# A two-level Strassen product: another order of the outer products, and the last two outputs stored in quarters

## The chip, the cores and the metric

The kernel runs on one core of a Trainium2 chip. The metric is the device time of one execution in microseconds (us), the median of several. The engines named here are TensorE (PE, matrix products, with its weight loads shown as PEld), VectorE (DVE, element-wise work), ScalarE (ACT), GpSimd (POOL) and SyncE (SP, which here only issues DMA transfers). A run before the change took 942.15 us (median of 3, from 942.0 to 943.19).

## The reference

A retention layer without softmax, then a feed-forward block with a squared ReLU. Everything is float32.

```python
# q, k, v: (8, 8, 576, 64)
scores = scale * np.matmul(q, k.transpose(0, 1, 3, 2))
ret = scores * Dmat[None, :, :, :]          # decay by position, zero above the diagonal
attn = np.matmul(ret, v)
x = attn.transpose(0, 2, 1, 3).reshape(4608, 512)
h = np.maximum(x @ w_in, 0.0)               # w_in: (512, 2048)
out = h * h @ w_out                         # w_out: (2048, 512)
```

The case is about the last line, called the second product here: g = h*h, 4608 tokens by 2048, times w_out, 2048 by 512.

## The kernel before, in words

Retention and the first product (x @ w_in) take the first 547 us, and the second product the rest. Tokens stand along the free dimension throughout, so outputs are computed transposed.

**The second product is Strassen's scheme in Winograd's form, twice, one inside the other.** One level replaces the eight products of a 2 x 2 block product by seven, listed in `PRODUCTS` (L27): A11·B11, S2·T2, S1·T1, A12·B21, S3·T3, S4·B22, A22·T4. S1 to S4 are sums of quarters of the left side: S1 = A21 + A22, S2 = S1 - A11, S3 = A11 - A21, S4 = A12 - S2. T1 to T4 are sums of quarters of the right side (the weights), made in earlier stages.

**Outer level.** The tokens are worked in six groups. A group has seven *steps*, one for each outer product, in the order of `OUTER` (L38), so there are N_K = 42 steps, k = 0 to 41, and j = k % 7 is the place in the group. Before, the order was S1, A11, S2, A12, S4, S3, A22. The left operand of a step is a buffer A(k) of 128 x 3072 elements, and there are four such buffers, used in turn (k % 4). A11, S1, A12, S3 and A22 were computed with the first product, are kept in DRAM (`g_dram`) and fetched by `fetch_g` in two halves, LOW and HIGH, one over the rows 0 to 3, the other over 4 to 7 of the buffer's eight. S2 and S4 are not kept: `made` (L969 to L976) subtracts two buffers that are there, in four quarters, each one DVE instruction of 768 elements per partition (L975). In the order of its list, quarter 0 is (LOW, RIGHT), 1 is (HIGH, RIGHT), 2 is (LOW, LEFT) and 3 is (HIGH, LEFT). For the inner level these are A21, A22, A11 and A12 of that operand.

**Inner level.** `inner(k, i)` is inner product i of step k: eight matmul passes of 128 x 192 in the trace (L1053), 1.30 us. The inner sums S1 to S4 are made by `inner_sum` (L992), each one DVE instruction of 768 elements. The products' results are combined from PSUM by DVE and ACT: p1 (ACT, L1060), u2 (DVE, L1062), p15 (L1064), then the four quarters of the step's result r (ACT L1066, DVE L1068, L1070, L1072).

**The order in the loop** (L1117 to L1149) is written by hand; each engine works its own list in that order. A step of the loop interleaves the first four inner products of step k with the last three of step k - 1. On PE it reads: inner(k,0), inner(k-1,4), inner(k,1), inner(k-1,5), inner(k,2), inner(k-1,6), inner(k,3), 9.1 us in all. The three passes of the inner loop (e = 0, 1, 2) are called thirds of a step below. DVE's list in a step is, third by third:

- e = 0: the quarter of r from inner(k-1,4); u2; what `extra(0)` holds; S1 of step k+1; the transposes of an output that leaves.
- e = 1: the quarter of r from inner(k-1,5); p15; S3 and S4 of step k; what `extra(1)` holds.
- e = 2: the quarter of r from inner(k-1,6); S2 of step k+1; the outer additions of step k-1; what `extra(2)` holds.

`extra` takes the quarters of `made` (the table `extras`, L1121) and, until they are used up, steps of `sums_0` (L1001), which loads, adds (L1016) and stores sums for one block of tokens that the first product left undone. At the end of a step SP gets the fetches of half a buffer for step k+3 and half for step k+4 (L1148, L1149).

**Outer sums and outputs.** `outer(k)` (L1087) adds r of a step into X, Y and Z, each 128 x 768 (L1093), seven additions in a group. A finished output quarter of the product leaves in the next step: `leave` (L1025) transposes it on DVE in blocks of 32 x 32 (L1030) into one of three buffers used in turn and issues its stores (L1038), four for each contiguous run of tokens, so eight for most outputs, on SP. For the last step `last_inner` (L1074) adds the inner products straight into the output and stores it in three pieces, on SP and ACT in turn; the output before it leaves whole, on both queues too.

Stores and fetches take one of eight semaphores in turn, whichever queue issues them, and each waits for the landing of the transfer that had that semaphore before it.

Of the kernel before, what the change touches and what calls it, by code (L numbers as in the profile page):

```python
# [9 lines left out]
F32 = mybir.dt.float32  # L10
# [3 lines left out]
ALU = mybir.AluOpType  # L14
# [12 lines left out]
PRODUCTS = (  # L27
    ("A11", "B11", "a"),
    ("S2", "T2", "b"),
    ("S1", "T1", "c"),  # L30
    ("A12", "B21", "a"),
    ("S3", "T3", "b"),
    ("S4", "B22", "c"),
    ("A22", "T4", "b"),
)
OPENS = {0, 1, 2}
CLOSES = {3, 5, 6}
OUTER = [PRODUCTS[j] for j in (2, 0, 1, 3, 5, 4, 6)]  # L38


@with_exitstack
def kernel(
# [33 lines left out]
    nc = tc.nc  # L76
# [13 lines left out]
    NP = len(PRODUCTS)  # L90
# [38 lines left out]
    room = const.tile([128, 15872], F32, name="room")  # L129
# [225 lines left out]
    for half in range(2):  # L355
        at = slice(CH * half, CH * half + CH)
# [270 lines left out]
    def fetch_w2(j):  # L627
        nc.sync.dma_start(w_out[j].rearrange("p m s f -> p m (s f)"), w2_dram[WO_SLOT[OUTER[j][1]], :, :, :])

# [304 lines left out]
    late2 = ctx.enter_context(tc.tile_pool(name="late2", bufs=2))  # L934
# [4 lines left out]
    TC = 3 * HT // 2  # L939
    NQ = TC // 2  # L940
    N_K = N_BLK * HT // TC * NP
# [2 lines left out]
    size = N_M * TC  # L944
    A_room = [late.tile([128, size], F32, name=f"a{j}") for j in range(2)] + [room[:, at:at + size] for at in (5888, 11776)]
    s_room = [late.tile([128, N_M * NQ], F32, name="s0"), room[:, 10240:10240 + N_M * NQ]]
    X, Y, Z = (room[:, at:at + 2 * TC].rearrange("p (e t) -> p e t", e=2) for at in (0, 2 * TC, 4 * TC))
    t_room = [room[:, at:at + 2 * TC].rearrange("p (a e c) -> p a e c", e=2, c=32) for at in (2304, 3072, 3840)]
    LOW, HIGH = slice(0, N_MQ), slice(N_MQ, N_M)
    LEFT, RIGHT = slice(0, NQ), slice(NQ, TC)  # L950

    def A(k):
        return A_room[k % 4].rearrange("p (m t) -> p m t", m=N_M)

    def runs(n, lo=0, hi=TC):

        while lo < hi:
            b, t = divmod(n * TC + lo, HT)
            w = min(HT - t, hi - lo)
            yield BLOCKS[b], t, lo, w  # L960
            lo += w

    def fetch_g(k, ms):

        if k < N_K and OUTER[k % NP][0] in G_KEPT:
            for b, t, c, w in runs(k // NP):
                nc.sync.dma_start(A(k)[:, ms, c:c + w], g_dram[b, G_KEPT.index(OUTER[k % NP][0]), :, ms, t:t + w])

    def made(k):  # L969

        if k >= N_K:
            return [None] * 4
        x, y = (k - 2, k - 1) if k % NP == 2 else (k - 1, k - 2)
        at = [(LOW, RIGHT), (HIGH, RIGHT), (LOW, LEFT), (HIGH, LEFT)]
        return [lambda m=m, t=t: nc.vector.tensor_tensor(A(k)[:, m, t], A(x)[:, m, t], A(y)[:, m, t], op=ALU.subtract)  # L975
                for m, t in at]  # L976

    def lefts(k):

        x = A(k)  # L980
        t = s_room[k % 2].rearrange("p (s m t) -> p s m t", s=2, m=N_MQ)
        return dict({f"S{e + 1}": t[:, e % 2, :, :] for e in range(4)},
                    A11=x[:, LOW, LEFT], A12=x[:, HIGH, LEFT], A21=x[:, LOW, RIGHT], A22=x[:, HIGH, RIGHT])
# [4 lines left out]
    def inner_sum(k, name):  # L988
        if 0 <= k < N_K:
            x = lefts(k)  # L990
            a, b, op = INNER[name]
            nc.vector.tensor_tensor(x[name], x[a], x[b], op=op)  # L992
# [3 lines left out]
    def bank(name):  # L996
        n_bank[0] += 1
        pool, tag = (ps_f, "f") if n_bank[0] % 8 < 3 else (ps_g, "g")
        return pool.tile([128, 512], F32, tag=tag, name=name)[:, 0:NQ]
# [22 lines left out]
    leaving = []  # L1022
    n_left = [0]

    def leave(k, o, h, e, es, lo, hi, both=False):  # L1025

        t = t_room[n_left[0] % 3]
        n_left[0] += 1
        for i in range(es.start, es.stop):
            nc.vector.transpose(t[:, 0:(hi - lo) // 32, i, :], o[:, i, lo:hi])  # L1030
        for b, at, c, w in runs(k // NP, lo, hi):
            row = b * TOK + h * HT + at
            to = out[row:row + w, e * HT:(e + 1) * HT].rearrange("(a r) (p e c) -> p r a e c", r=32, e=2, c=32)[:, :, :, es, :]
            lo_ = (c - lo) // 32
            for p in range(4):
                own = slice(32 * p, 32 * p + 32)
                queue_ = nc.scalar if both and p % 2 else nc.sync
                queue_.dma_start(to[p], t[own, lo_:lo_ + w // 32, es, :])  # L1038

    def inner(k, i):  # L1040

        n, j = divmod(k, NP)
        if i == 0:
            small = late3.tile([128, 3, NQ], F32, tag="small", name="small")
            r = (Y, X)[j] if j < 2 else late2.tile([128, 2, TC], F32, tag="r", name="r")
            state[k] = dict(r=r, lefts=lefts(k), p1=small[:, 0, :], u2=small[:, 1, :], p15=small[:, 2, :])
        s = state[k]
        left, right, to = PRODUCTS[i]
        if i in OPENS:
            s[to] = bank(f"o_{to}")  # L1050
        p = s[to]
        for m in range(N_MQ):
            nc.tensor.matmul(p, lhsT=w_out[j][:, m, WO_SLOT[right], :], rhs=s["lefts"][left][:, m, :],  # L1053
                             start=(i in OPENS and m == 0), stop=(i in CLOSES and m == N_MQ - 1),
                             skip_group_check=True)
        r = s["r"]
        if k == N_K - 1 and i >= 3:
            last_inner(s, i, p)
        elif i == 0:
            nc.scalar.copy(s["p1"], p)  # L1060
        elif i == 1:
            nc.vector.tensor_tensor(s["u2"], p, s["p1"], op=ALU.add)  # L1062
        elif i == 2:
            nc.vector.tensor_tensor(s["p15"], p, s["p1"], op=ALU.add)  # L1064
        elif i == 3:
            nc.scalar.copy(r[:, 0, LEFT], p)  # L1066
        elif i == 4:
            nc.vector.tensor_tensor(r[:, 1, RIGHT], p, s["p15"], op=ALU.add)  # L1068
        elif i == 5:
            nc.vector.tensor_tensor(r[:, 1, LEFT], p, s["u2"], op=ALU.add)  # L1070
        else:
            nc.vector.tensor_tensor(r[:, 0, RIGHT], p, s["p1"], op=ALU.add)  # L1072

    def last_inner(s, i, p):  # L1074
        add = lambda to, x, y: nc.vector.tensor_tensor(to, x, y, op=ALU.add)
        at = {3: (0, LEFT), 4: (1, RIGHT), 5: (1, LEFT), 6: (0, RIGHT)}
        place = lambda i: Z[:, at[i][0], at[i][1]]
        own = {4: s["p15"], 5: s["u2"], 6: s["p1"]}
        if i == 3:
            for e in (4, 5, 6):  # L1080
                add(own[e], own[e], place(e))
        add(place(i), p, own.get(i, place(3)))
        e, t = at[i]
        if i != 3:
            leave(N_K - 1, Z, 1, 0, slice(0 if i == 5 else e, e + 1), t.start, t.stop, True)

    def outer(k):  # L1087

        n, j = divmod(k, NP)
        r = state.pop(k)["r"]  # L1090
        for to, x, with_ in {2: [(Z, r, X), (Y, Y, Z)], 3: [(X, r, X)], 4: [(X, r, Y)], 5: [(Y, r, Y), (Z, r, Z)],
                             6: [(Z, r, Z)]}.get(j, []):
            nc.vector.tensor_tensor(to, x, with_, op=ALU.add)  # L1093
        if j >= 3:
            o, h, e = {3: (X, 0, 0), 4: (X, 0, 1), 5: (Y, 1, 1), 6: (Z, 1, 0)}[j]
            leaving.append(lambda: leave(k, o, h, e, slice(0, 2), 0, TC, k == N_K - 2))


    n_last = 0
# [17 lines left out]
    for k in range(N_K + 1):  # L1117
        j = k % NP
        if j in (0, 2):
            parts = made(k + 2)  # L1120
        extras = {0: [0, 1], 1: [2, None, 3], 2: [0, 1, 2], 3: [None, 3]}.get(j, [])  # L1121
        assert k + 4 < N_K - NP or next(steps_0, None) is None

        def extra(e):
            own = [parts[extras[e]]] if e < len(extras) and extras[e] is not None else []
            for f in own + [next(steps_0, None)]:
                f and f()

        if k < N_K:
            inner(k, 0)  # L1130
        for e in range(3):
            if k > 0:
                inner(k - 1, 4 + e)
            if e == 2:
                inner_sum(k + 1, "S2")
                if 0 < k < N_K:
                    outer(k - 1)
            if k < N_K:
                inner(k, 1 + e)
            if e == 1:  # L1140
                inner_sum(k, "S3")
                inner_sum(k, "S4")
            extra(e)
            if e == 0:
                inner_sum(k + 1, "S1")
                while leaving:
                    leaving.pop(0)()
        fetch_g(k + 3, HIGH)  # L1148
        fetch_g(k + 4, LOW)  # L1149


def _decays(B, H, S, D):
# [43 lines left out]
```

## Time and profile before

| what | us |
|---|---|
| median of the runs | 942.15 |
| the profiled execution, its own time | 941.51 |
| its span in the profile | 939.8 |
| PE busy in the span | 925.0 |
| DVE busy in the span | 759.9 |
| ACT busy in the span | 346.9 |
| L992, inner sums, mean of one | 0.948 |
| L975, quarters of S2 and S4, mean of one | 0.949 |
| L1093, outer additions, mean of one | 0.950 |
| L1030, transposes of 384 elements, mean of one | 0.554 |
| L1038, issue of one store on SP, median | 0.438 |
| L1038, from issue to landing, median | 1.8 |

The span runs from the first to the last instruction of the program; 1.7 us of the execution's time lie around it. A row of a timeline gives the start, the length, the engine, the line, what it writes and reads, the size and how many instructions were merged; in brackets the idle time of the engine before it and the instruction that ended it. SPq and ACTq are DMA issues. Consecutive DVE instructions overlap a little: a 768-element one lasts 0.95 us, and the next can start 0.87 us after it.

### The profile page before, as it was taken

To read this page: it belongs to the slowest core of one execution; us is meant where nothing else is said; L and a number is where in the kernel's file an instruction comes from. 1 tells how busy PE (TensorE), PEld (TensorE's weight loads), DVE (VectorE), ACT (ScalarE), POOL (GpSimd) and SP (SyncE) were. 2 spreads that over 40 slices of the span, in tenths; PEclk is the share of its full clock that TensorE was granted. 3 is DMA by queue.
4 is the path that set the end of the run, shared out by engine and by line. 5 is a ranking of instruction groups with operands and counts; after the bars stand their busy time and mean duration, and the time that the engine had idled before them with its cause. 6 is when DMAs were issued, how large, how long until landed. Compare 5 with 4: busy or idle time off the path is not lost.

```text
span 939.8 us, 21110 instructions
## 1 busy us (share of the span) xinstructions
PE 925.0 (98%) x8548; PEld 830.6 (88%) x8548; DVE 759.9 (81%) x1235; ACT 346.9 (37%) x789; POOL 83.3 (9%) x82
## 2 busy tenths in 40 slices
PE   9999999999999999999999999999999999999996
PEld 7554888888888888888888899999999999999996
DVE  5978699879798888888856587887888887887975
ACT  3557767676676676766611110000000000000000
POOL 3222021111121111211000000000000000000000
PEclk9999999999999999999999999999999999999999
DMA  9998575686578666863559985566566556555523
GB/s 228 214 267 215 155 193 152 193 288 180 155 197 274 190 174 176 282 183 115 200 195 352 380 298 180 155 179 198 155 181 179 158 167 185 129 173 148 135 70 65
DMA packets 297313, 181.30 MB, mean 193 GB/s; under 512 B 194304, under 2 KB 270208, under 8 KB 296320
## 3 DMA queue, kind: packets, MB, share of 16 engines
q1 hardware_dynamic: 293008, 179.04, 66.0%
q8 instruction: 67, 1.10, 0.5%
q10 hardware_dynamic: 4208, 0.92, 0.5%
q14 instruction: 30, 0.25, 0.1%
HBM read 109.39 MB, written 70.52 MB: 191 GB/s over the span
## 4 chain that ended last, share of the span: by engine, by line
PE 93%; DVE 4%; DMA 1%; ACT 1%; issue 0%; DVEq 0%; SPq 0%
PE h_b L717 17%; PE o_b L1053 17%; PE h_a L717 12%; PE o_c L1053 11%; PE h_c L717 11%; PE o_a L1053 11%; PE h_ps L679 6%; PE x_ps L576 3%; PE sc_ps L482 2%; PE x_ps L611 1%; PE u_ps L570 1%; DMA k_ld<-in_k_dram 1%; DVE w L244 0%; PE t_ps L447 0%; DVE room L992 0%
## 5 line engine op out<-in xcount | busy, mean ns | idle before, releaser
L717 PE MATMUL h_b<-room,w 128*128 128x256 f32 x768 | 181.9, 380 | 0.9 <-DVE room L736 0.9
L433 ACT COPY qk<-flip 32x256 f32<-32x256 f32 x432 | 173.8, 402 | 6.8
L717 PEld LDWEIGHTS h_b<-room,w 128*128 128x128 f32 x768 | 145.5, 190 | 21.9 <-DVE room L736 2.3
L717 PE MATMUL h_a<-room,w 128*128 128x256 f32 x512 | 123.9, 385 | 0.0
L717 PE MATMUL h_c<-room,w 128*128 128x256 f32 x512 | 121.0, 379 | 0.0
L717 PEld LDWEIGHTS h_c<-room,w 128*128 128x128 f32 x512 | 97.3, 190 | 13.2
L717 PEld LDWEIGHTS h_a<-room,w 128*128 128x128 f32 x512 | 95.0, 190 | 13.7
L1053 PE MATMUL o_b<-room,w 128*128 128x192 f32 x496 | 90.8, 326 | 0.8 <-DVE room L992 0.8
L1066 ACT COPY r<-o_a 128x192 f32<-128x192 f32 x29 | 9.2, 319 | 217.0 <-PE o_a L1053 217.0
L1053 PEld LDWEIGHTS o_b<-room,w 128*128 128x128 f32 x496 | 82.3, 190 | 1.1 <-DVE room L992 1.1
L724 DVE SCALAR_TENSOR_TENSOR room<-room 128x512 f32<-128x512 f32 x96 | 67.9, 708 | 3.3
L398 POOL TENSOR_TENSOR q_ld<-q_ld,dv 128x512 f32<-128x512 f32 x34 | 39.8, 1171 | 289.9 <-DMA q_ld<-in_q_dram 237.7
L1053 PE MATMUL o_a<-a,w 128*128 128x192 f32 x352 | 62.6, 326 | 0.0
L1053 PE MATMUL o_b<-s,w 128*128 128x192 f32 x336 | 61.5, 326 | 0.0
L1053 PE MATMUL o_c<-s,w 128*128 128x192 f32 x336 | 61.5, 326 | 0.0
L1053 PE MATMUL o_c<-room,w 128*128 128x192 f32 x336 | 61.5, 326 | 0.0
L679 PE MATMUL h_ps<-room,w 128*128 128x512 f32 (+1 forms) x152 | 57.7, 532 | 0.7 <-DVE w L244 0.7
L1053 PEld LDWEIGHTS o_a<-a,w 128*128 128x128 f32 x352 | 58.1, 190 | 0.1
L1053 PE MATMUL o_a<-room,w 128*128 128x192 f32 x320 | 56.9, 326 | 0.0
L1053 PEld LDWEIGHTS o_c<-s,w 128*128 128x128 f32 x336 | 55.8, 190 | 0.0
L1053 PEld LDWEIGHTS o_c<-room,w 128*128 128x128 f32 x336 | 55.8, 190 | 0.0
L1053 PEld LDWEIGHTS o_b<-s,w 128*128 128x128 f32 x336 | 55.8, 190 | 0.0
(116 smaller groups left out, 1415.2 us busy)
## 6 DMA issues: line engine op xcount, KB each, us to landing
g_dram<-room SPq DMA_DIRECT2D x164, 256.0 KB, 3.8
a<-g_dram SPq DMA_DIRECT2D x30, 512.0 KB, 4.8
room<-g_dram SPq DMA_DIRECT2D x28, 512.0 KB, 5.0
w_dram<-w SPq DMA_DIRECT2D x28, 448.0 KB, 4.8
w<-w_dram SPq DMA_DIRECT2D x7, 1792.0 KB, 9.6
q_ld<-in_q_dram SPq DMA_DIRECT2D x64, 128.0 KB, 4.2
w<-in_moe_w_in_dram SPq DMA_DIRECT2D x16, 512.0 KB, 6.2
w<-in_moe_w_out_dram SPq DMA_DIRECT2D x64, 128.0 KB, 3.3
```

Of the source, the lines that this page charges most:

```text
L398: engine.tensor_tensor(t, t, dv[:, heads, at:at + 1].to_broadcast(list(t.shape)), op=ALU.mult)
L433: nc.scalar.copy(*moves.pop(0)[2:])
L482: nc.tensor.matmul(st[i]["sc"][e][rows(h), hp, :], lhsT=st[i]["kT"][rows(e), hp, t], rhs=st[i]["qT"][rows(e), hp, t], start=True, stop=Tru ...
L570: return [lambda hp=hp, e=e, b=b: nc.tensor.matmul(u[rows(e), hp, :], lhsT=loaded[i][1][rows(h), 2 * hp + e, :], rhs=st[i]["vs"][rows(h), ...
L576: return [lambda hp=hp, e=e, b=b: nc.tensor.matmul(x_at(hp, e, b, h), lhsT=s["vs"][rows(h), head(hp, e), :], rhs=s["ret"][rows(h), e, hp, ...
L611: m = nc.tensor.matmul(x_at(hp, e, b, h), lhsT=u[rows(e), hp, :], rhs=s["qT"][rows(e), hp, CH * h:CH * h + CH], start=clears(b, e), stop=F ...
L679: nc.tensor.matmul(p, lhsT=w[:, c, :], rhs=xT[0][:, c, :].rearrange("p (h t) -> p h t", h=2)[:, lo:hi, at[0]:at[1]], start=(c == 0), stop= ...
L717: nc.tensor.matmul(p[:, mm, :], lhsT=w[:, c, :], rhs=xs[n][right][:, c, :], start=(j in OPENS and mm == 0 and c == 0), stop=(j in CLOSES a ...
L724: nc.vector.scalar_tensor_tensor(t, t, 0.0, t, op0=ALU.max, op1=ALU.mult)
L1053: nc.tensor.matmul(p, lhsT=w_out[j][:, m, WO_SLOT[right], :], rhs=s["lefts"][left][:, m, :], start=(i in OPENS and m == 0), stop=(i in CLO ...
L1066: nc.scalar.copy(r[:, 0, LEFT], p)
```

## The change

1. `OUTER` is reordered: S1, A11, S2, A12, **S3, A22, S4**. S4 is now A(k-3) - A(k-4), made over S2 in S2's own buffer. The outer additions and the output that each step finishes follow (C22 after S3, C21 after A22, C12 after S4).
2. The quarters of `made` stand in other places. S2: quarter 0 in the last third of j = 0, quarters 1, 2 and 3 in the three thirds of j = 1 (before: 0 and 1 in the first two thirds of j = 0, 2 and 3 in the first and last third of j = 1). S4: quarters 0 and 2 at the end of j = 2, 1 at the end of j = 3, 3 in the first third of j = 4.
3. Both halves of S3 are fetched at the end of j = 1, since its buffer holds S1 until S2 is made.
4. X and Y swap their buffers from group to group.
5. `leave` transposes with one instruction where two stood. The last two outputs are both added from PSUM by inner products and stored in pieces, the last but one in four and the last in three, on SP and ACT; for the last step the three additions of kept sums are made after inner products 1 and 2, not at 3.

```diff
-OUTER = [PRODUCTS[j] for j in (2, 0, 1, 3, 5, 4, 6)]
+OUTER = [PRODUCTS[j] for j in (2, 0, 1, 3, 4, 6, 5)]
...
-    X, Y, Z = (room[:, at:at + 2 * TC].rearrange("p (e t) -> p e t", e=2) for at in (0, 2 * TC, 4 * TC))
+    O_ = [room[:, at:at + 2 * TC].rearrange("p (e t) -> p e t", e=2) for at in (0, 2 * TC, 4 * TC)]
...
-        x, y = (k - 2, k - 1) if k % NP == 2 else (k - 1, k - 2)
+        x, y = (k - 2, k - 1) if k % NP == 2 else (k - 3, k - 4)
...
+    def XYZ(k):
+        n = k // NP
+        return O_[n % 2], O_[1 - n % 2], O_[2]
...
-        for i in range(es.start, es.stop):
-            nc.vector.transpose(t[:, 0:(hi - lo) // 32, i, :], o[:, i, lo:hi])
+        to, at = t[:, 0:(hi - lo) // 32, es, :], o[:, es, lo:hi]
+        nc.vector.transpose(to.rearrange("p a e c -> p e a c"), at.rearrange("p e (a c) -> p e a c", c=32))
...
-                queue_ = nc.scalar if both and p % 2 else nc.sync
-                queue_.dma_start(to[p], t[own, lo_:lo_ + w // 32, es, :])
+                queues[p % len(queues)].dma_start(to[p], t[own, lo_:lo_ + w // 32, es, :])
...
-        if k == N_K - 1 and i >= 3:
-            last_inner(s, i, p)
+        if k >= N_K - 2 and i >= 3:
+            last_inner(k, s, i, p)
...
+        if k == N_K - 1 and i in (1, 2):
+            last_sums(k, s, (5,) if i == 1 else (4, 6))
+
+    PLACES = {3: (0, LEFT), 4: (1, RIGHT), 5: (1, LEFT), 6: (0, RIGHT)}
...
+    def last_sums(k, s, which):
+        for i in which:
+            own = s[{4: "p15", 5: "u2", 6: "p1"}[i]]
+            nc.vector.tensor_tensor(own, own, place(k, i), op=ALU.add)
+
+    def last_inner(k, s, i, p):
+        x = place(k, i)
+        if i == 3 and k == N_K - 2:
+            last_sums(k, s, (4, 5, 6))
+        nc.vector.tensor_tensor(x, p, x if i == 3 else s[{4: "p15", 5: "u2", 6: "p1"}[i]], op=ALU.add)
+        last = k == N_K - 1
+        o, h, e = (XYZ(k)[1], 0, 1) if last else (XYZ(k)[2], 1, 0)
+        at, t = PLACES[i]
+        if not last or i != 3:
+            queues = {3: (nc.sync,), 4: (nc.scalar,)}.get(i, (nc.sync, nc.scalar)) if not last else (nc.sync, nc.scalar)
+            leave(k, o, h, e, slice(0 if last and i == 5 else at, at + 1), t.start, t.stop, queues)
...
-        for to, x, with_ in {2: [(Z, r, X), (Y, Y, Z)], 3: [(X, r, X)], 4: [(X, r, Y)], 5: [(Y, r, Y), (Z, r, Z)],
-                             6: [(Z, r, Z)]}.get(j, []):
+        if k >= N_K - 2:
+            return
+        X, Y, Z = XYZ(k)
+        for to, x, with_ in {2: [(Z, r, X), (Y, Y, Z)], 3: [(X, r, X)], 4: [(Z, r, Z), (X, r, Y)], 5: [(Z, r, Z)],
+                             6: [(Y, r, Y)]}.get(j, []):
...
-            parts = made(k + 2)
-        extras = {0: [0, 1], 1: [2, None, 3], 2: [0, 1, 2], 3: [None, 3]}.get(j, [])
+            parts = made(k + 2 if j == 0 else k + 4)
+        extras = {0: [[], [], [0]], 1: [[1], [2], [3]], 2: [[], [], [0, 2]], 3: [[], [], [1]], 4: [[3]]}.get(j, [])
...
+        if j == 1:
+            fetch_g(k + 3, LOW)
         fetch_g(k + 3, HIGH)
-        fetch_g(k + 4, LOW)
+        if j != 0:
+            fetch_g(k + 4, LOW)
```

More of the change, by code (lines that the diff above doesn't have):

```diff
@@ L1023, with leave @@
     n_left = [0]
-    def leave(k, o, h, e, es, lo, hi, both=False):
+    def XYZ(k):
+        n = k // NP
+        return O_[n % 2], O_[1 - n % 2], O_[2]
+    def leave(k, o, h, e, es, lo, hi, queues=(nc.sync,)):
         t = t_room[n_left[0] % 3]
         n_left[0] += 1
-        for i in range(es.start, es.stop):
-            nc.vector.transpose(t[:, 0:(hi - lo) // 32, i, :], o[:, i, lo:hi])
+        to, at = t[:, 0:(hi - lo) // 32, es, :], o[:, es, lo:hi]
+        nc.vector.transpose(to.rearrange("p a e c -> p e a c"), at.rearrange("p e (a c) -> p e a c", c=32))
         for b, at, c, w in runs(k // NP, lo, hi):
@@ L1044, in inner @@
             small = late3.tile([128, 3, NQ], F32, tag="small", name="small")
-            r = (Y, X)[j] if j < 2 else late2.tile([128, 2, TC], F32, tag="r", name="r")
+            r = XYZ(k)[1 - j] if j < 2 else late2.tile([128, 2, TC], F32, tag="r", name="r")
             state[k] = dict(r=r, lefts=lefts(k), p1=small[:, 0, :], u2=small[:, 1, :], p15=small[:, 2, :])
@@ L1072, in inner, with place @@
             nc.vector.tensor_tensor(r[:, 0, RIGHT], p, s["p1"], op=ALU.add)
[L1074 to L1085, printed above, removed]
+        if k == N_K - 1 and i in (1, 2):
+            last_sums(k, s, (5,) if i == 1 else (4, 6))
+    PLACES = {3: (0, LEFT), 4: (1, RIGHT), 5: (1, LEFT), 6: (0, RIGHT)}
+    def place(k, i):
+        return XYZ(k)[2 if k % NP == 5 else 1][:, PLACES[i][0], PLACES[i][1]]
+    def last_sums(k, s, which):
[13 more added lines that the diff above has]
+            leave(k, o, h, e, slice(0 if last and i == 5 else at, at + 1), t.start, t.stop, queues)
     def outer(k):
@@ L1090, in outer @@
         r = state.pop(k)["r"]
-        for to, x, with_ in {2: [(Z, r, X), (Y, Y, Z)], 3: [(X, r, X)], 4: [(X, r, Y)], 5: [(Y, r, Y), (Z, r, Z)],
-                             6: [(Z, r, Z)]}.get(j, []):
+        if k >= N_K - 2:
[3 more added lines that the diff above has]
+                             6: [(Y, r, Y)]}.get(j, []):
             nc.vector.tensor_tensor(to, x, with_, op=ALU.add)
         if j >= 3:
-            o, h, e = {3: (X, 0, 0), 4: (X, 0, 1), 5: (Y, 1, 1), 6: (Z, 1, 0)}[j]
-            leaving.append(lambda: leave(k, o, h, e, slice(0, 2), 0, TC, k == N_K - 2))
+            o, h, e = {3: (X, 0, 0), 4: (X, 1, 1), 5: (Z, 1, 0), 6: (Y, 0, 1)}[j]
+            leaving.append(lambda: leave(k, o, h, e, slice(0, 2), 0, TC))
     n_last = 0
@@ L1119 @@
         if j in (0, 2):
-            parts = made(k + 2)
-        extras = {0: [0, 1], 1: [2, None, 3], 2: [0, 1, 2], 3: [None, 3]}.get(j, [])
+            parts = made(k + 2 if j == 0 else k + 4)
+        extras = {0: [[], [], [0]], 1: [[1], [2], [3]], 2: [[], [], [0, 2]], 3: [[], [], [1]], 4: [[3]]}.get(j, [])
         assert k + 4 < N_K - NP or next(steps_0, None) is None
         def extra(e):
-            own = [parts[extras[e]]] if e < len(extras) and extras[e] is not None else []
+            own = [parts[x] for x in extras[e]] if e < len(extras) else []
             for f in own + [next(steps_0, None)]:
```

## The prediction

> **What bounds the kernel now.** I read the page first, then the waits of TensorE (PE) and VectorE (DVE) in the second product (540 to 940 us), then the stage table, then one stretch of the timeline, and last the end.
>
> ```profile
> span 939.8 us, 21110 instructions
> PE 925.0 (98%) x8548; PEld 830.6 (88%) x8548; DVE 759.9 (81%) x1235; ACT 346.9 (37%) x789; POOL 83.3 (9%) x82
> ...
> PE o_b L1053 <- DVE room L992: 0.8, 1, 0.8
> PE o_b L1053 <- DVE room L1075: 0.6, 1, 0.6
> ...
> DVE small L1062 <- PE o_b L1053: 35.7, 41, 1.5
> ```
>
> PE is the bound. In the whole second product it waits twice, 0.85 us near the start and 0.58 us at the very end; DVE is the engine that waits, once in each of the 42 outer steps, for PE's second product of the step.
>
> ```profile
> 600.00:700.00 100.00, 100.00 (x617) 100.00 (x616) 84.81 (x145) 7.01 (x22) 0.00 (x0) 1.00 0.60 170
> 700.00:800.00 100.00, 100.00 (x618) 100.00 (x617) 82.33 (x140) 7.02 (x22) 0.00 (x0) 1.00 0.62 176
> ```
>
> The columns are the stretch, its length, busy time of PE, PEld, DVE, ACT and POOL, the clock, the DMA share and GB/s. PE is busy for all of 600 to 900, at full clock, so nothing taken off DVE there can make the kernel faster; a wait given to PE is added in full. DVE has 15 us free in 100, but not evenly, and the timeline of step 15 (681.00 to 690.10; step k begins at 544.5 + 9.1k) shows how little is free inside one step:
>
> ```profile
> 685.17 0.36 DVE L1062 TENSOR_TENSOR small<-o_b,small 128x192 f32<-128x192 f32 x1 [0.69 <-PE o_b L1053]
> 685.45 0.95 DVE L975 TENSOR_TENSOR a<-room 128x768 f32<-128x768 f32 x1
> 686.31 0.42 DVE L1016 TENSOR_TENSOR g<-g 128x256 f32<-128x256 f32 x1
> 686.65 0.95 DVE L992 TENSOR_TENSOR s<-a 128x768 f32<-128x768 f32 x1
> 687.52 1.03 DVE L1030 STREAM_TRANSPOSE room<-room 128x384 f32<-128x384 f32 x2
> 688.47 0.32 DVE L1070 TENSOR_TENSOR room<-o_c,small 128x192 f32<-128x192 f32 x1
> 688.72 0.34 DVE L1064 TENSOR_TENSOR small<-o_c,small 128x192 f32<-128x192 f32 x1
> 688.98 1.80 DVE L992 TENSOR_TENSOR room<-room 128x768 f32<-128x768 f32 x2
> ...
> 690.10 1.46 PE L1053 MATMUL o_a<-a,w 128*128 128x192 f32 x8
> ```
>
> From 685.17 DVE runs without a gap. The pair at 688.98 is S3 and S4 of step 15; it ends at 690.78, after PE has begun step 16 at 690.10. Step 16 is the S2 product, and its first product reads the A11 quarter of the S2 that DVE makes (L975). Here that quarter was made at 685.45, in time.
>
> The end has its own limit, the issue of the stores:
>
> ```profile
> 914.87 22.94 SPq L1038 DMA_DIRECT2D out_dram<-room  x28
> ...
> 930.04 1.57 PE L1053 MATMUL o_b<-a,w 128*128 128x192 f32 x8 [0.58 <-DVE room L1075]
> ...
> 930.43 6.01 ACTq L1038 DMA_DIRECT2D out_dram<-room  x12
> ```
>
> PE's last product ends at 931.61, SP issues until 937.81, and the last store lands about 1.1 us later.
>
> **What the Trainium skill says.** "Trainium Architecture — The Big Picture", section "Inside one NeuronCore": every engine has its own instruction stream, and engines meet only through semaphores. "Perfetto Trace Analysis", section "Tensor Engine Instruction (MATMUL, LD_WEIGHTS)": "ACT/DVE/GPSIMD are strict FIFO". Together: a quarter is made where it stands in DVE's stream, however early its inputs are there; the unbroken chain above agrees. "DMA: Bandwidth & Descriptors", section "Issuing engines are not separate DMA queues": issuing from a second engine saves only the issuing sequencer's time. The trace agrees in kind: SP's store issues stand 0.47 us apart, and that is what bounds the end.
>
> **The change part by part.** *New order of the outer products.* PE's work and weights stay the same in number and size. The outer additions stay seven in a group of seven steps (step j=4 gets two, j=5 one). 0 on PE.
>
> *S2 made in other steps.* L975 makes S2 in four quarters. Before: quarters 0 and 1 in step j=0, quarter 2 in the first third of j=1, quarter 3 at its end. After: quarter 0 at the end of j=0, quarter 1 in the first third of j=1, **quarter 2, the A11 quarter, in the second third**, which in DVE's built order is behind S3 and S4 of that step; quarter 3 at its end. The first third of j=1 holds the same pieces as before (one quarter, in some groups a sum L1016, S1, the transposes), so the starts of S4 in the trace of before carry over. S1 now reads the quarter just made: a dependent 768-element pair starts 0.98 apart where an independent one starts 0.87 apart, +0.11, unless the L1016 sum lies between. Then quarter 2 starts 0.87 after S4, takes 0.95, and PE follows 0.05 later (as at 556.10 after a sum ended at 556.04). PE wants it 9.10 into the step. S4 starts, in the six j=1 steps, at 7.85, 8.50, 8.84, 8.84, 8.50 and 8.50 into the step (the third is 689.84):
> group 0: 7.85 + 0.87 + 0.95 + 0.05 = 9.72, wait 0.62 (S4 itself follows PE there, so the 0.11 is absorbed);
> groups 1, 4, 5: 8.50 + 0.11 + 1.87 = 10.48, wait 1.38 each, 4.14;
> groups 2, 3, with the sum between: 8.84 + 1.87 = 10.71, wait 1.61 each, 3.22.
> Sum 7.98. After both waits of before, the eight passes took 1.57 instead of 1.46, so a restart costs 0.1: six times, 0.6. Total **+8.6**. Nothing regains it, since PE has no other gap to lose. Behind the waiting matmul stands all of PE; DVE catches up meanwhile, so the next need, S2's own inner sum, is met 1 us early.
>
> *The first step.* The 0.85 wait at 556.10 was for an inner sum of step 1 that stood behind two quarters in the short step 0. With both out of its way (2 x 0.87) it is 0.9 us early. **-0.95** with the restart.
>
> *S4 made in place over S2*, its quarters at the ends of j=2 and j=3 and in j=4, used in j=6: two steps of slack. 0.
>
> *S3 fetched whole at the end of j=1* (before: half a step's data at each end). Both halves are due at S1 in step 3, 4.45 us in. In group 2, the latest, SP reaches its fetch 4.44 us into step 16 (694.54); there 0.79 MB landed in 5.25 us. Twice that at the 260 GB/s seen with several fetches queued is 1.5 + 6.0, landing 2.8 into step 17, 1.6 early. 0; if that cover goes, S1 waits, and PE only after DVE's own slack, at most some 2 us in two groups.
>
> *One transpose instead of two* (L1030): the pair takes 0.95 of DVE's time, and the 512-element transposes of the first stage 0.70, or 1.09 ns an element and 0.14; 768 elements give 0.98 long, 0.9 between starts. 0; the four-dimensional pattern is not in the trace: between -0.1 and twice as long, I take 0.
>
> *The end.* The last two outputs leave in quarters: 24 stores become 48 from 921.8 on. DVE adds the first quarter of the last-but-one output at 921.4 (after two outer additions and three small ones that begin at 918.35), so SP starts issuing at 921.8 instead of 923.1 and has 30 stores: 29 x 0.48 = 13.9, and 0.95 in which its fifth waits for an earlier store on ACT's queue, since each store as built waits for the landing of the eighth before it. Last issue 936.6, landed 1.55 later, 938.2, where before it was 938.96. PE's 0.58 wait and its restart go (the add before it is no longer behind 2.8 us of sums), but that does not set the end. Bounds: if only the last quarter's add, transpose and stores counted, 934.6, so -4.4; if stores proceed at the 2.8 per us seen from 930.4 to 939, 45 of them take 16.1 us to 939.5, +0.5. I take **-0.7**.
>
> Sum: +8.6 - 0.95 - 0.7 = +6.95. The profiled execution took 941.51 (span 939.8 and 1.7 around it), so 948.5; the median of before's runs lies 0.64 above it, and on that scale the forecast is **949.0**.
>
> **The rivals.** *Hidden quarter (not slower).* If quarter 2 were ready before step j=2 begins, only the two gains remain: 942.15 - 0.95 - 0.7 = 940.5. It decides once DVE's chain to that quarter is shorter by 0.6 to 1.6 us. For it: DVE is idle 15% of the time. Against it: even with no lag S3 starts 6.98 into the step, after the p15 read that waits for PE, and 6.98 + 2 x 0.87 + 0.95 = 9.67 is past 9.10. *Late fetch of S3.* If the three half fetches of j=1 (2.4 MB) share the DMA engines rather than land in turn, S3 lands up to 3 us late, in perhaps four groups with about 1 us left over for PE each: 953. For it: DMA busy 0.6, up to 0.95 around the fetches. Against: landings came in order of issue. *Slow transpose.* Twice as long puts 0.95 ahead of quarter 2 in five groups: +4.75, 953.7. Against: the first stage's transposes are as fast per element with strides.
>
> **How the numbers follow.** Forecast 0.77, hidden quarter 0.04, late fetch 0.12, slow transpose 0.07. The forecast's own bounds: the end from -4.4 to +0.5 about the -0.7 taken gives 945.3 to 950.2, the six waits 0.15 each, 0.9. Range 945.8 to 951.8, which leaves out most of the last two rivals and the first. 0.2% is 1.9 us, about what a measurement of this kernel can tell from no change: slower by more 0.95, within 0.02, faster 0.03.
>
> **What would show it.** Among the waits of PE, a line of some 8 us in six waits for the subtraction that made S2 (L975), 1.3 to 1.7 us each but the first; no wait at 556; no wait for DVE in the last product; stores on both queues from about 922 plus the shift; PE busy time unchanged. Wrong if that line is missing, if DVE waits for the g loads of S3, or if the last stretch after PE's end is longer than the 7.4 us (931.6 to 939.0) of before.

## The result, and the profile after

The changed kernel takes 947.73 us (median of 4 runs, 946.83 to 948.84), where before took 942.1 beside it. The ratio is 1.0058, with a 95% interval of 1.004 to 1.0075: 3.8 to 7.1 us slower. The prediction was 949.0 with a range of 945.8 to 951.8. The profiled execution took 948.84 us.

The head of the page, of the kernel after:

```profile
span 947.1 us, 21105 instructions
PE 926.3 (98%) x8548; PEld 831.0 (88%) x8548; DVE 761.8 (80%) x1217; ACT 346.5 (37%) x788; POOL 82.7 (9%) x82
```

PE has the same 8548 matmuls, and is busy for 926.3 us where it was busy for 925.0. The span has grown by 7.3 us, so most of it is time in which PE stands idle. The waits of PE in the second product (who waited, for whom, us in total, times, the longest):

```profile
PE o_a L1056 <- DVE a L975: 3.7, 3, 1.4
PE o_a L1056 <- DVE room L975: 3.0, 3, 1.4
```

Both waits of before are gone. Six new ones stand there, all for L975, the subtraction that makes S2 in quarters. The stage table (columns as before: stretch, length, PE, PEld, DVE, ACT, POOL, clock, DMA share, GB/s) shows that they are spread over the whole product and that PE's clock is full:

```profile
600.00:700.00 100.00, 97.45 (x599) 96.86 (x598) 81.66 (x132) 7.00 (x22) 0.00 (x0) 1.00 0.58 163
700.00:800.00 100.00, 98.62 (x607) 98.33 (x607) 81.54 (x132) 7.01 (x22) 0.00 (x0) 1.00 0.63 178
```

The first stretch has two of the waits (1.17 + 1.38, what PE lacks to 100 us), the second one (1.38). DVE is no busier than it was, and still has 18 us free in 100. The timeline shows why that doesn't help. First DVE in step 15, then PE at the start of step 16, both of the kernel after:

```profile
687.38 0.36 DVE L1065 TENSOR_TENSOR small<-o_b,small 128x192 f32<-128x192 f32 x1 [1.01 <-PE o_b L1056]
687.66 0.95 DVE L975 TENSOR_TENSOR a<-room 128x768 f32<-128x768 f32 x1
688.52 0.42 DVE L1016 TENSOR_TENSOR g<-g 128x256 f32<-128x256 f32 x1
688.86 0.95 DVE L992 TENSOR_TENSOR s<-a 128x768 f32<-128x768 f32 x1
689.73 0.97 DVE L1034 STREAM_TRANSPOSE room<-room 128x768 f32<-128x768 f32 x1
690.62 0.32 DVE L1073 TENSOR_TENSOR room<-o_c,small 128x192 f32<-128x192 f32 x1
690.87 0.34 DVE L1067 TENSOR_TENSOR small<-o_c,small 128x192 f32<-128x192 f32 x1
691.13 1.80 DVE L992 TENSOR_TENSOR room<-room 128x768 f32<-128x768 f32 x2
692.86 0.95 DVE L975 TENSOR_TENSOR a<-room 128x768 f32<-128x768 f32 x1
```

```profile
693.86 1.57 PE L1056 MATMUL o_a<-a,w 128*128 128x192 f32 x8 [1.38 <-DVE a L975]
```

DVE's free microsecond lies ahead of u2 (687.38), where DVE waits for PE. From there it runs without a gap, and the quarter that PE needs is the last thing in the row, behind S3 and S4. It ends at 693.81, and PE starts 0.05 us later. The 1.57 us for eight passes, where the other products take 1.46, is the restart.

At the end of the kernel, the stores (SP and ACT) and the waits of DVE for buffers, of the kernel after:

```profile
923.19 21.91 SPq L1041 DMA_DIRECT2D out_dram<-room  x38
```

```profile
930.72 14.09 ACTq L1041 DMA_DIRECT2D out_dram<-room  x18
```

```profile
DVE room L1034 <- DMA out_dram<-room: 3.9, 2, 2.9
```

PE's last product, in the same kernel:

```profile
937.68 1.46 PE L1056 MATMUL o_b<-a,w 128*128 128x192 f32 x8
```

PE ends at 939.15, SP issues stores until 945.10, and the span ends at 947.1, 7.93 us after PE. This stretch from PE's end to the end of the span is called the tail below; before, it was 8.17 us. Inside it, DVE now waits for landed stores before it can transpose into one of the three buffers.

The sum of the two traces, from PE's first matmul of the second product: PE takes 390.69 us where it took 384.32 (6.36 more, unrounded), and the tail is 0.24 shorter, together +6.12. (The second product also begins 1.17 us later in this profile. Over the profiles of all kernels below, it begins between 546.46 and 549.73 without any change in the first stage. From here on PE's time in the second product and the tail are compared, and the medians beside them.)

### The profile page after: what moved, and what is told of

It is laid out like the page before. It is cut to its first block, busy times and chain, and to the rows that moved or that the text cites. A ratio compares the mean times of both kernels' runs of the same rounds, so it can differ in the third digit from the quotient of the medians.

```text
span 947.1 us, 21105 instructions
## 1 busy us (share of the span) xinstructions
PE 926.3 (98%) x8548; PEld 831.0 (88%) x8548; DVE 761.8 (80%) x1217; ACT 346.5 (37%) x788; POOL 82.7 (9%) x82
## 4 chain that ended last, share of the span: by engine, by line
PE 88%; DVE 6%; DMA 3%; issue 1%; SPq 1%; ACT 0%; DVEq 0%
PE h_b L717 17%; PE o_b L1056 14%; PE h_a L717 12%; PE h_c L717 11%; PE o_a L1056 10%; PE o_c L1056 9%; PE h_ps L679 6%; PE x_ps L576 3%; PE sc_ps L482 2%; PE x_ps L611 1%; PE u_ps L570 1%; DMA room<-g_dram 1%; DVE s L992 1%; DVE room L992 1%; DMA a<-g_dram 1%
## 5 line engine op out<-in xcount | busy, mean ns | idle before, releaser
L1056 PEld LDWEIGHTS o_a<-room,w 128*128 128x128 f32 x320 | 52.7, 190 | 3.9 <-DVE room L975 3.9
```

## The experiments

Each kernel is compared with before, which ran on the same chip, in five rounds (there is no e6).

**e1: two quarters earlier.** The change as it is, with each of quarters 1 and 2 one place earlier, so that quarter 2 stands ahead of S3 and S4:

```diff
-        extras = {0: [[], [], [0]], 1: [[1], [2], [3]], ...
+        extras = {0: [[], [], [0, 1]], 1: [[2], [], [3]], ...
```

> The changed kernel with the quarters of S2 placed differently: 0 and 1 at the end of j=0, 2 (the A11 quarter) in the first third of j=1, 3 at its end. Late-quarter theory: the six waits of PE for L975 (7.7 us by the starts of the matmuls, and 0.1 us of restart each) go entirely, nothing takes their place: 947.7 - 8.3 = 939.4, faster than the kernel before. Rival (DVE is too full in j=0 and j=1, the wait only moves): the inner sum S2 or the quarters of r come late instead, PE waits for L992 or L1071, and the time stays at 942 to 946.

Measured: 939.62 us, ratio 0.9981 (0.997 to 0.9992). PE's time in the second product is 382.36 us, and it never waits in it. DVE in the same step of this kernel:

```profile
683.51 0.95 DVE L975 TENSOR_TENSOR a<-room 128x768 f32<-128x768 f32 x1
684.37 0.42 DVE L1016 TENSOR_TENSOR g<-g 128x256 f32<-128x256 f32 x1
684.71 0.95 DVE L992 TENSOR_TENSOR s<-a 128x768 f32<-128x768 f32 x1
685.58 0.97 DVE L1034 STREAM_TRANSPOSE room<-room 128x768 f32<-128x768 f32 x1
```

The L975 at 683.51 is quarter 2. PE starts the product that reads it at 688.16, 3.7 us after it ended. So the whole loss in the product is the place of these two quarters in DVE's list, among others that are all the same; e2 tells the share of the late quarter.

**e2: the late quarter alone, in the kernel before.** In the kernel before, quarter 2 is moved from the first third of j = 1 to the second, with nothing else:

```diff
-        extras = {0: [0, 1], 1: [2, None, 3], 2: [0, 1, 2], 3: [None, 3]}.get(j, [])
+        extras = {0: [0, 1], 1: [None, 2, 3], 2: [0, 1, 2], 3: [None, 3]}.get(j, [])
```

> The kernel before with one edit: the A11 quarter of S2 moved from the first to the second third of j=1; quarters 0 and 1 stay in j=0. Late-quarter theory: the price is set by what DVE has ahead of the quarter. With no other quarter in the first third S4 starts 7.85 into the step (7.98 where the L1016 sum stands there), so the wait is 0.62 in four groups and 0.74 in two, with restarts 4.56 in all: 942.1 + 4.6 = 946.7. Rival (a quarter in the second third costs what it did in the changed kernel, 8.3 us, whatever stands ahead): 950.4. Rival (the late fetch or the order of the outer products is the cause): no change, 942.1.

Measured: 946.52 us, ratio 1.0049 (1.0036 to 1.0062). PE's time grows from 384.32 to 388.89, 4.57 us. The waits of PE in this kernel:

```profile
PE o_a L1053 <- DVE room L975: 1.5, 3, 0.6
PE o_a L1053 <- DVE a L975: 1.5, 3, 0.6
PE o_b L1053 <- DVE room L992: 0.8, 1, 0.8
PE o_b L1053 <- DVE room L1075: 0.6, 1, 0.6
```

The place of quarter 2 makes the waits without the new order, the new fetches or the new transposes. But for the first, they are 0.7 to 0.8 us shorter than in the kernel after, and here quarter 1, another 0.87 us of DVE, is not in j = 1. The size fits, so that part of the waits is put down to it; no run moves quarter 1 alone.

**e3: the first step's wait put back.** e1, with the first step's quarters where before had them:

```diff
+        if k == 0:
+            extras = [[0], [1], []]
```

> e1_quarter_early with quarters 0 and 1 of the first S2 back in the first two thirds of step 0, as in the kernel before. Theory: the wait of step 1 for its inner sum S2 returns, 1.0 us by the starts of the matmuls and 0.1 of restart: 1.1 us above e1_quarter_early. Rival (that wait came from transfers at the start of the product, not from the quarters): the same time as e1_quarter_early.

Measured: 941.25 us, ratio 0.999 (0.9982 to 0.9998). PE's time is 383.48, 1.12 us above e1's, and the first of the two waits of before returns at its place (the medians of e1 and e3 have overlapping intervals; the traces decide here):

```profile
PE o_b L1056 <- DVE room L992: 0.8, 1, 0.8
```

**e4: the end with shorter waits for a buffer.** e1, with a fourth buffer for transposed outputs, and the output of step 39 stored on SP and ACT:

```diff
-... for at in (2304, 3072, 3840)]
+... for at in (2304, 3072, 3840, 4608)]
...
-        t = t_room[n_left[0] % 3]
+        t = t_room[n_left[0] % 4]
...
-            leaving.append(lambda: leave(k, o, h, e, slice(0, 2), 0, TC))
+            leaving.append(lambda: leave(k, o, h, e, slice(0, 2), 0, TC, (nc.sync, nc.scalar) if k == N_K - 3 else (nc.sync,)))
```

> e1_quarter_early with a fourth buffer for transposed outputs and the output before the last two (C22) stored on SP and ACT in turn. Theory: in the changed kernel the end is set by DVE waiting for a buffer (3.9 us in two waits for stores) and by SP's 30 issues; without both, the last store lands 2 to 4 us after what PE's end allows less than now: 2 to 4 us below e1_quarter_early. Rival (the rate at which stores land sets the end, whatever the queues and buffers): within 0.7 us of e1_quarter_early.

Measured: 939.39 us, ratio 0.9977 (0.9966 to 0.9988). DVE's wait for landed stores fell from 3.9 to 1.1 us:

```profile
DVE room L1034 <- DMA out_dram<-room: 1.1, 2, 0.8
```

The tail fell by 0.54 us only, from 7.92 to 7.38, and the intervals of e1 and e4 overlap. The theory fell. The last transpose now ends 0.81 us after PE instead of 3.72, but SP still issues stores until 5.40 us after PE. DVE's waits at the end cost nothing, because the queues had older stores to issue meanwhile. Nor did the four stores that went to ACT bring SP's end forward by their issue time, some 1.9 us at 0.47 each: from the first quarter's stores on, SP waited 2.9 us for landings of earlier stores in this kernel, 0.9 in e1.

**e5: two transposes again.** e1, with the loop of before in `leave`:

```diff
+        for i in range(es.start, es.stop):
+            nc.vector.transpose(t[:, 0:(hi - lo) // 32, i, :], o[:, i, lo:hi])
```

> The kernel with the quarter early (e1), but with one transpose for each half of an output again, as before the change. Theory (the transposes lie in DVE's slack): two of 0.55 us in place of one of 0.98 cost DVE 0.12 us for each whole output and nothing of the time: second product 382.4 us on PE, no wait of PE, 939.6 us. Rival (one transpose over both halves is what holds up or relieves DVE): at least one wait of PE in steps in which an output leaves, or a second product that differs from 382.4 by 1 us or more.

Measured: 941.01 us, ratio 0.9985 (0.9976 to 0.9994), which can't be told from e1's 0.9981. PE's time is e1's, 382.36, without a wait, so once the quarter is early, the transposes of the product's steps lie in DVE's slack. The tail of the profiled run is 8.65 us, 0.73 more than e1's; whether two more instructions or the timing of the stores did that, this one profile doesn't settle.

**e7: the last output but one whole again.** e1, with that output added as one addition in `outer` and stored whole:

```diff
-        if k >= N_K - 2 and i >= 3:
+        if k == N_K - 1 and i >= 3:
             last_inner(k, s, i, p)
...
-        if k >= N_K - 2:
+        if k == N_K - 1:
             return
...
-            leaving.append(lambda: leave(k, o, h, e, slice(0, 2), 0, TC))
+            leaving.append(lambda: leave(k, o, h, e, slice(0, 2), 0, TC, (nc.sync, nc.scalar) if k == N_K - 2 else (nc.sync,)))
```

> The quarter early (e1), and the last output but one added whole and stored whole one step later on two queues, as before the change. It has 24 stores for the last two outputs where e1 has 40. Theory (the tail is a count of stores: SP and ACT issue one in 0.47 us each; the quarters gain nothing at the end, and the wait of 0.74 us at the end of before went because one addition of 768 fewer stands ahead of the last sums): second product 382.4 us, tail 7.7 to 8.4 us where e1 has 7.92, time 939.4 to 940.1 us. Rival (the prediction's: storing by quarters is what gains 0.7 at the end): 0.7 us or more of it comes back, as a wait of PE near the end or as a tail of 8.6 us and more, 940.3 us and more.

Measured: 939.78 us, ratio 0.9978 (0.9971 to 0.9986). PE's time is 382.36, the tail 8.20. The wait of 0.74 us at the end of before doesn't come back. So it was not the quarters that removed it. What is left as its cause is the new order, with one outer addition of 768 elements fewer ahead of the last sums, or the earlier place of those sums; these two were not run apart. Quarters shorten the tail by 0.28 us in the profile, and the medians show nothing of that.

**e8: the quarters added, but stored at once and whole.** e1, with 8 stores for the last output but one in place of 24:

```diff
-        if not last or i != 3:
+        if not last and i == 6:
+            leave(k, o, h, e, slice(0, 2), 0, TC, (nc.sync, nc.scalar))
+        if last and i != 3:
```

> The quarter early (e1); the last output but one is added by quarters, but stored whole, on two queues, as soon as its last quarter is added: 8 stores of 64 or 32 KB in place of 24 of 24 KB and less, some 1.5 us before PE's last matmul of the step that follows. Theory (the tail is the number of stores still to be issued at 0.47 us each on SP and ACT): 16 fewer stores are 8 fewer on each queue, of which some 5 stood in the backlog at the end: tail 5.5 to 6.5 us where e1 has 7.92, time 937.2 to 938.4. Rival (a fixed time from the last addition to the last landing, or bytes and not stores): tail 7.5 to 8.2, time 939.4 to 940.

Measured: 939.63 us, ratio 0.9979 (0.9971 to 0.9986), tail 7.44 us: 0.5 us less than e1's, where 1.4 to 2.4 were expected, and by the medians no faster than e1. What stood in the way is in the waits of SP's own queue, of this kernel from 922 us on:

```profile
SPq L1041 <- DVE room L1093: 4.3, 1, 4.3
SPq L1041 <- DMA out_dram<-room: 3.6, 3, 2.8
```

The first line is only the time in which nothing is there to store. The second is a wait for landings, and one of 2.8 us stands in the middle of the end:

```profile
923.93 2.90 SPq L1041 DMA_DIRECT2D out_dram<-room  x6
929.64 6.25 SPq L1041 DMA_DIRECT2D out_dram<-room  x12
```

SP is idle from 926.82 to 929.64. Until 927.99, when DVE's transpose ends, it has nothing to store; for the last 1.65 us data is ready. Its next store has its turn on a semaphore whose last user is the first of ACT's stores of that output, and in the program as built ACT's stores of that output come first in the turn, apparently because SP has the eight of step 39 ahead of its own:

```profile
928.02 6.41 ACTq L1041 DMA_DIRECT2D out_dram<-room  x12
```

It lands 1.55 us later, at 929.58, and SP follows at 929.64. So two queues that share eight semaphores in turn can hold each other up, when one is ahead of the other in the program's order. Counting stores was too coarse. The last transpose in turn waits 2.40 us for its buffer, whose stores stand on SP:

```profile
933.21 0.38 DVE L1034 STREAM_TRANSPOSE room<-room 128x192 f32<-128x192 f32 x1 [2.40 <-DMA out_dram<-room]
```

**e9: the queues in balance, and merged stores.** e8, with step 39's output on both queues, and the last output's 64-token pieces in two stores instead of four:

```diff
+            if k == N_K - 1 and w == 64:
+                for a in range(2):
+                    queues[a].dma_start(to.rearrange("p r a e c -> a p r e c")[a], t[:, lo_ + a, es, :])
+                continue
...
-            leaving.append(lambda: leave(k, o, h, e, slice(0, 2), 0, TC))
+            leaving.append(lambda: leave(k, o, h, e, slice(0, 2), 0, TC, (nc.sync, nc.scalar) if k == N_K - 3 else (nc.sync,)))
```

> As e8, and the output before is stored on SP and ACT in turn instead of on SP alone, and the last output's pieces of 64 tokens leave in 2 stores in place of 4. Theory (the number of stores): 4 fewer on SP before the end and 1 fewer on each queue in the tail: tail 0.3 to 1.0 us below e8's, time 936.5 to 938. Rival (e8's fixed time): tail as e8's and e1's, 7.5 or more.

Measured: 938.29 us, ratio 0.9966 (0.9953 to 0.9979), tail 6.20 us, 1.24 below e8's; the intervals of e8 and e9 overlap. ACT's stores in this kernel's end:

```profile
922.96 9.07 ACTq L1045 DMA_DIRECT2D out_dram<-room  x12
...
932.07 1.33 ACTq L1041 DMA_DIRECT2D out_dram<-room  x1
933.50 0.82 ACTq L1045 DMA_DIRECT2D out_dram<-room  x2
```

A merged store (L1041 here) holds ACT for 1.33 us, and its twin holds SP for 0.68. The two stores it replaces take 0.44 each on ACT, and 0.32 and 0.39 on SP (in e11). So the merging may well have cost time; e11 tells.

**e10: e9 with a fourth buffer,** by the first two edits of e4.

> e9 with a fourth buffer for what is transposed, so that the last transpose doesn't wait until stores have landed (1.23 us of idle DVE in e9's trace, when SP and ACT had nothing else left to issue). Theory (in e9 the last of the tail is this buffer): the last four stores are issued some 1.0 to 1.2 us earlier, tail 4.9 to 5.4 us where e9 has 6.20, second product 382.4 us, time about 937.1 us. Rival (as in e4, where a fourth buffer took 2.8 us of idle DVE away and the tail shrank by 0.5 only, since stores were still queued): tail 5.8 to 6.2, time 938.3 as e9.

Measured: 938.47 us, ratio 0.9966 (0.9951 to 0.9981), tail 6.20, the same as e9's. DVE's last transpose ends 0.82 us after PE instead of 2.00, and nothing follows from it. The expectation misread e9: SP and ACT were not out of work while DVE waited, they were issuing the two merged stores.

**e11: the balance alone.** e9 without its merged stores, that is e8 with the last line of e9's diff.

> e8 with step 39's output on both queues, without the merged stores of e9. Theory (the gain of e9 came from the balance: SP no longer stands for 2.8 us until a store of ACT's has landed, since both queues take the eight semaphores in turn in step): tail 6.0 to 6.5 us, SP's waits for landings below 1 us where e8 has 3.6, time as e9, about 938.3 us. Rival (it came from the merged stores): tail 7.0 us or more, time as e8, about 939.6.

Measured: 937.67 us, ratio 0.995 (0.993 to 0.9969), tail 5.72 us, 1.72 below e8's and 0.48 below e9's. The waits of SP's queue, as for e8:

```profile
SPq L1041 <- DVE room L1093: 7.4, 2, 4.1
...
SPq L1041 <- DMA out_dram<-room: 0.3, 2, 0.2
```

The hole of 2.8 us is gone, the whole gain of e9 is the balance, and in the profiles the merged stores cost 0.5 of it. The medians tell e11 from e8 (the intervals do not overlap), but not from e9. In e8 to e11 PE's time is always 382.36. e11 is the fastest kernel of the study: 2.9 to 6.6 us faster than before (0.31 to 0.7% of 942.74), where the change as it stands is slower by 3.8 to 7.1. The Trainium skill ("DMA: Bandwidth & Descriptors", section "Issuing engines are not separate DMA queues") says that a second issuing engine saves only time on the issuing sequencer, which is usually small. In this case the moved stores brought something else: four stores of step 39's output, moved from SP to ACT, took 1.72 us off the tail, and it was not their issue time, since e8's SP was through with them at 926.82, before the next data was there. What went was the 1.65 us in which SP had data and waited for a landing. The balance alone does not ensure it: e4 makes the same move, with a fourth buffer besides, where the last output but one leaves in quarters, and its tail fell by 0.54 us.

## Why the prediction was right, and where it was off

| term of the sum | predicted | in the traces | shown by |
|---|---|---|---|
| six waits for quarter 2 of S2 | 7.98 | 7.70 | e1, e2 |
| six restarts | 0.6 | 0.62 | after |
| the first step | -0.95 | -1.12 | e3 |
| the end | -0.7 | -1.08 | after; e7 in part |
| fetch of S3, S4, the single transpose, in the steps | 0 | 0 (see the waits) | after, e5 |
| sum | +6.95 | +6.12 | |

*The waits.* The rows of the wait view give 6.7 us, and the difference has a reason that concerns every reading of this kind. Idle time before a matmul is counted from the modelled end of the matmul before it, and that lies 0.16 us after the next should have started. Judged by its start, the product at 693.86 is 1.38 + 0.16 = 1.54 us late (1.55 unrounded). By group the six are 0.61, 1.33, 1.55, 1.54, 1.33 and 1.33 us, where the prediction had 0.62, 1.38, 1.61, 1.61, 1.38 and 1.38. The 0.05 to 0.07 less in each of five groups is the single transpose, which the prediction put at nothing: it stands ahead of quarter 2 there, and what follows it starts 0.89 us after it begins, where with the pair it was 0.95. The prediction said that the step's list on DVE, read from before, with the moved quarter inserted, gives the start of PE; e1 takes the quarter out of that place (and quarter 1 out of the step) and the waits go, and e2 puts it there alone and they come. e2's rows sum to 3.0 us, and with 0.16 and a restart of 0.10 for each of six to 4.56; PE's time grew by 4.57.

*The first step.* e3 measures it, 1.12 us. In before the product at 556.10 was 1.01 late by its start, and 0.10 for the restart; the prediction took the idle time of 0.85 as the wait and so missed the 0.16.

*The end.* The forecast of what sets the end fits the trace of after: SP issues 30 stores from 930.06 on, one directly behind another but for one wait of 0.93 us (0.95 forecast), and the last begins 14.6 us after the first (14.8 forecast). (The prediction's "24 stores become 48" doesn't count alike: the last two outputs go from 24 stores to 40, and 48 has step 39's eight too.) What it had half wrong is the worth of the wait of 0.58 us, which it let go for nothing. In the terms of the table 0.85 of the 1.08 us is that wait (0.74 by its start) with its restart, and 0.24 the shorter tail. e7 has neither quarters nor the wait, its tail is only 0.28 longer than e1's, and by the medians it is no slower. So without the quarters, the going of the wait is worth some 0.8 us in the traces (0.85, less the 0.03 by which e7's tail exceeds that of before). e5's tail, 0.73 longer in one profile, leaves open whether the single transpose has a share in the end too.

*What was costed at nothing.* No wait of DVE for the fetched sums appears in the trace after, so the late fetch did not happen (DMA was busier around the fetches of before than the 0.95 that the prediction read: 0.99 from 763 to 765 us). One transpose of 768 elements takes 0.97 us, against 0.98 estimated, so the slow transpose did not happen either. The hidden quarter is the kernel e1: the price given to it, 940.5, is near the 939.62 measured, and it is what the kernel would have been with these two quarters one place earlier.

The forecast was 1.3 us above the median (its sum, 941.51 + 6.95 + 0.64, is 949.1, where it says 949.0). Of this 0.8 is the sum of the terms above; the rest is within what medians of four runs leave open, since the interval of the ratio spans 3.3 us.

## What to carry to other kernels

When an engine works a list in a fixed order, a spare 18% of it says nothing about one instruction: find the step in which the other engine needs its result, add up the list from the last point where this engine waited, and see whether it is done by then. A prerequisite of the next step goes ahead of sums that are due later; here that cost PE nothing (e1). At the end of a kernel, count the stores on each issuing queue from the first that queues up; a shorter wait of the computing engine there brought nothing here while the queue that ends last was busy issuing (e10) or itself waiting for landings (e4). And where queues share semaphores, look for a queue that waits for another's store, as in e8; feeding both in step removed it in e11.

## What was not expected of the hardware

- A store that covers all 128 partitions with single rows of 64 elements held its queue for 0.68 us on SP and 1.33 us on ACT (e9), where stores of 32 partitions take 0.32 to 0.44 at the same place (e11). The two cost more issue time, 2.0 us, than the four they replaced, 1.6. ACT's began at 932.07, while SP's ran until 932.57, so part of the 1.33 may be a wait for the other queue; no run settles that.
- A queue stood for 2.8 us, the last 1.65 of them with data ready, until a store of the other queue had landed (e8), since both take the same eight semaphores in turn.
- PE's restart after a wait cost 0.10 us in all eight cases of before and after, by the starts of the matmuls, whether PE was late by 0.6 or by 1.5 us.
- PE's time in the second product is the same to 0.01 us in all eight profiles without a wait (382.36), while its start, with the same program ahead of it, differs by 2.3 us among them (546.46 to 548.75).
